# Load times in a planner's model, the place of an operand split, and when weights are decoded

## The chip, the cores and the metric

The kernel runs on one core of a Trainium2 chip. The metric is device time in microseconds (us), less is better. TensorE (PE) multiplies and transposes through PSUM, VectorE (DVE), ScalarE (ACT) and GpSimd (POOL) do elementwise work, SyncE (SP) issues DMAs. Each engine takes its instructions in the order in which the program lists them, and each instruction waits for the semaphores of what it needs.

## What is computed

A recurrence over 768 steps for 4 x 8 heads with a 40x40 state, then two feed-forward layers on its 3072 x 320 output:

```python
for t in range(S):
    y[:, :, t] = np.einsum('bhd,bhde->bhe', rt, state)
    Sa = np.einsum('bhde,bhe->bhd', state, at)
    state = state * wt[:, :, None, :] - np.einsum('bhd,bhe->bhde', Sa, bt) + np.einsum('bhd,bhe->bhde', vt, kt)
# first layer: h = x @ w_in (320 x 1024); softmax times h; layer norm; @ w_out (1024 x 320)
# second layer: h = x @ w_in (320 x 2048); g = max(h, 0) + alpha * min(h, 0); g @ w_out (2048 x 320)
```

The weights of both layers come as 64-bit floats.

## The kernel before

**Two parts.** The recurrence runs in 24 slots `g`, each a chunk of 32 steps of all heads; two chunks make one of 12 windows `w`. Slot g does `stage_x`, `stage_u`, `stage_st`, `stage_s` for its chunk and `stage_uf`, `stage_g2`, `stage_y` for the one before. For every four slots a triangular inverse is prepared: `gen1` (matmuls `pg`, masks into `XS`), 28 small dependent VectorE steps between transposes (`inverse`), then two groups of small matmuls (`pv`, `pn`). `slot_tasks` puts the last of it into the slot with c4 = g % 4 = 3. The first layer follows three and four slots behind the recurrence, from a queue of small pieces: `mm1` (16 pieces of `h`), `tr1`, `mm2` (8 pieces of `po`), `tr2`. After slot 23 comes a tail, ordered by the string TAIL, which finishes the first layer while the second layer runs for window 0 (`s` is a step of it, `w` loads weights, `n t u a b o` are pieces of the first layer). The last part runs the second layer for windows 1 to 11 in six groups of two windows (the last has one): per pair of steps `mm3` (`ph`), VectorE `gt`, ScalarE `gh`, POOL `gll`, and `mm4` (`acc`) two steps later.

**The order is written by a planner.** While the program is built, a model keeps a time `now[0]` for TensorE and one for each of ScalarE, VectorE and POOL (`free`). `note` advances TensorE's time by a booked price. `until` waits in the model for a key: meanwhile it pops pieces of the first layer from the queue, or filler matmuls (`zero`, in the early slots `busy`), whose product nobody reads. `pace` adds such work where the matmul columns of the last stretch are few. `fill` gives VectorE work from five lists when it is free in the model. Loads are booked as landed `DMA` = 3.5 us after they are asked for. The resulting order is kept on PE, ACT, DVE and POOL in the slots; SP's order is not written by the planner.

**Decoding of weights.** `w1_tasks` (11 pieces) and `w2_tasks` (28) load a piece of 64-bit words into a tile `raw` of a pool of two buffers (line 912). `decode_steps` turns it into fp32: VectorE masks (lines 877, 878), ScalarE conversions (881, 882), VectorE sign and low word (885, 889), then a product on VectorE or POOL (898), and for the second layer a store to `wd` or `od` in DRAM (947), from which `load_w` reads later. `pump` keeps at most two loads ahead and starts a piece when `lane["due"]` allows it: 11 at the start, then per slot NC[g % 4], NL[g % 4] in the last four slots.

**Moves.** `x_move` stores the recurrence's output `Y` to `xd` (line 751) and loads it again as `xt` in the layout of the first layer (752, 753). `tr2` transposes the first layer's output into PSUM, ScalarE rounds it to fp32r (high part), VectorE subtracts (low part, 856 and 857), and the five slices go to `x2_d` with one store (865). The last part loads them straight into its operand tile (1268).

Of the kernel before, what the change touches and what calls it, by code (L numbers as in the profile page):

```python
# [25 lines left out]
NC, NL = (1, 2, 2, 2), (2, 2, 2, 0)  # L26
# [6 lines left out]
TAIL = "s2 n0 w2 t0 s1 u0 a0 w3 b0 s1 n1 w4 o0 s1 t1 s1 u1 a1 w5 s1 b1 s1 n2 o1 s1 w6 t2 s1 u2 a2 x w7 s1 b2 s1 n3 o2 s1 t3 s1 u3 b3 s2 o3"  # L33
PLAIN_WT = {'gen00': 0.44, 'gen20': 1.8, 'tr1': 0.19}
LAT, PL, DMA = 0.1, 0.25, 3.5
# [10 lines left out]
def tile_kernel(ctx: ExitStack, tc: tile.TileContext, w_fm, a0_fm, a_fm, kb_fm, r_fm, v_fm, v_tm,  # L46
# [26 lines left out]
    x2_d = [dr.tile([128, 5, 256], F32R, name=f"x2d{w}") for w in range(NW)]  # L73
# [86 lines left out]
    st = {}  # L160
# [79 lines left out]
    def note(dt, n, r=0):  # L240
        page[0] += r
        if page[0] >= PAGE and not plain():
            page[0] -= PAGE
            t, page[1] = page[1] + FETCH, max(now[0], page[1] + FETCH)
            while now[0] < t:
                note(min(0.1, t - now[0]), 0)
        now[0] += dt
# [117 lines left out]
    def load_a(g):  # L365
# [8 lines left out]
        put(("a_in", g))(max(now[0], free["P"]) + DMA)  # L374
# [369 lines left out]
    def x_move(w):  # L744
# [7 lines left out]
        nc.sync.dma_start(out=f32(xt[:, 0:4]), in_=xd[w][0:n4].rearrange("(k p) t -> p k t", p=128))  # L752
        nc.sync.dma_start(out=f32(xt[:, 4]), in_=xd[w][n4:])


# [89 lines left out]
    def tr2(t):  # L845
# [6 lines left out]
        x2 = m1.tile([128, 5, 128], F32R, name="x2")  # L852
        hi = x2[:, 0:4, :].rearrange("p (a b) t -> p a b t", b=2)

        def low():
            nc.vector.tensor_tensor(out=hi[:, :, 1], in0=pt[:, 0:2], in1=f32(hi[:, :, 0]), op=ALU.subtract)
            nc.vector.tensor_tensor(out=x2[64:128, 4], in0=pt[0:64, 2], in1=f32(x2[0:64, 4]), op=ALU.subtract)

        def high():
            nc.scalar.copy(out=hi[:, :, 0], in_=pt[:, 0:2])  # L860
            nc.scalar.copy(out=x2[0:64, 4], in_=pt[0:64, 2])

        def end(u):
            wring[bk] = u
            nc.sync.dma_start(out=f32(x2_d[w][:, :, i * 128:i * 128 + 128]), in_=f32(x2[:]))
        chain(now[0] + PL, [("A", 0.64, high), ("V", 0.74, low)], end)


# [39 lines left out]
    def piece(src, dst=None, scales=(), eng="V", end=lambda o: []):  # L908

        n = src.shape[1] * src.shape[2]  # L910
        raw = rawp.tile([128, 1024], U32, name="raw")[:, 0:2 * n]
# [52 lines left out]
    def pump():  # L964

        while lane["tasks"] and lane["taken"] < over() + 2:
            lane["next"].append((lane["tasks"].pop(0)(), now[0] + DMA))
# [266 lines left out]
    def early_w():  # L1234
# [8 lines left out]
        for t, a, z in zip(st["x20"], (0, 4), (4, 5)):  # L1243
            nc.sync.dma_start(out=f32(t), in_=f32(x2_d[0][:, a:z] if z > a + 1 else x2_d[0][:, a]))

    def phase2(p2):
# [18 lines left out]
        def load_x(ws, t):  # L1265
# [378 lines left out]
```

## Time and profile before

| | us |
|---|---|
| median of 3 runs | 1111.93 |
| lowest and highest | 1100.17, 1115.77 |
| profiled execution, device time | 1114.18 |
| its span, first to last instruction | 1112.4 |

| engine | busy us | share of the span |
|---|---|---|
| PE | 1010.7 | 91% |
| PEld (weight loads) | 790.0 | 71% |
| DVE | 653.8 | 59% |
| ACT | 526.5 | 47% |
| POOL | 298.7 | 27% |

A matmul's end is modelled in the profile, so a busy PE is not a PE at its peak. The granted clock is that of TensorE as a share of full speed. An "idle before" names the engine's idle time just ahead of an instruction and what ended it.

### The profile page before, as it was taken

The page shows a single profiled execution, that of the slowest core. Times are in us where ns is not written, and L with a number is a line of the kernel's source. Part 1 is how long each engine was busy: PE and PEld are TensorE (multiplying, and loading weights), DVE is VectorE, ACT ScalarE, POOL GpSimd, SP SyncE. Part 2 cuts the span into 40 slices and gives each one's busy share as a digit, 9 for nine tenths or more (in the row PEclk, how much of TensorE's full clock was granted, in tenths as well). Part 3 has the DMA queues.
Part 4 walks back from the last instruction along what each step waited for, and adds up shares of the span by engine and source line. Part 5 has one row for each costly group of instructions (what it writes and reads, how often), then busy time and mean ns, then how long its engine had stood idle before and what let it go on. Part 6 is the DMA issues. An engine that isn't in the chain of part 4 may idle for free.

```text
span 1112.4 us, 36263 instructions
## 1 busy us (share of the span) xinstructions
PE 1010.7 (91%) x15862; PEld 790.0 (71%) x15862; DVE 653.8 (59%) x1242; ACT 526.5 (47%) x1177; POOL 298.7 (27%) x352
## 2 busy tenths in 40 slices
PE   6589979699879799799999899999999999999997
PEld 3346647476657557666777577688899988999997
DVE  8837977587668677576868353554434443334443
ACT  1226727367567537475667477658412121212121
POOL 6400131012212221122202113143333333333332
PEclk9668979699998899798899899999999999999999
DMA  7504343534453523462453433356202020201010
GB/s 175 161 28 113 81 113 96 132 103 113 147 150 102 151 69 100 116 156 84 112 151 100 142 97 84 94 190 199 59 1 71 1 71 1 72 1 48 1 25 15
DMA packets 103145, 103.55 MB, mean 93 GB/s; under 512 B 37828, under 2 KB 80580, under 8 KB 102980
## 3 DMA queue, kind: packets, MB, share of 16 engines
q1 hardware_dynamic: 102980, 101.16, 33.1%
q8 instruction: 126, 2.06, 0.8%
q14 instruction: 39, 0.32, 0.1%
HBM read 75.71 MB, written 25.43 MB: 91 GB/s over the span
## 4 chain that ended last, share of the span: by engine, by line
PE 68%; DMA 9%; DVE 9%; ACT 6%; issue 5%; POOL 2%; SPq 1%; DVEq 0%; POOLq 0%; ACTq 0%
PE ph L1279 15%; PE po L837 8%; PE h L767 6%; PE acc L1299 5%; PE acc L1297 5%; PE acc L1298 5%; DMA raw<-in_w_out_dram 3%; PE busy L339 3%; PE py L724 3%; PE zero L297 2%; PE pst L665 2%; PE pf L652 2%; PE pg L701 2%; PE pss L685 2%; DMA kbf<-in_kb_fm_dram 2%
## 5 line engine op out<-in xcount | busy, mean ns | idle before, releaser
L802 DVE TENSOR_SCALAR gt<-ph,al 128x512 f32<-128x512 f32 (+1 forms) x112 | 75.3, 674 | 194.3 <-PE ph L1279 194.2
L1286 POOL TENSOR_TENSOR gll<-gt,gh 128x512 fp32r<-128x512 f32 (+1 forms) x112 | 128.2, 1146 | 226.9 <-ACT gh L1285 225.0
L1285 ACT CAST gh<-gt 128x512 fp32r<-128x512 f32 (+1 forms) x112 | 62.4, 558 | 251.3 <-DVE gt L803 215.3
L837 PE MATMUL po<-wo,ln 128*128 128x320 f32 x384 | 131.6, 477 | 0.9 <-ACT ln L829 0.8
L767 PE MATMUL h<-w1h,xt 128*128 128x512 f32 x240 | 94.9, 452 | 0.0
L837 PEld LDWEIGHTS po<-wo,ln 128*128 128x128 f32 x384 | 71.7, 201 | 26.4 <-issue 4.5
L1297 PE MATMUL acc<-w2h,gh 128*128 128x320 f32 x288 | 88.8, 308 | 0.0
L1298 PE MATMUL acc<-w2l,gh 128*128 128x320 f32 x288 | 88.8, 308 | 0.0
L1299 PE MATMUL acc<-w2h,gll 128*128 128x320 f32 x288 | 88.7, 308 | 0.0
L898 POOL TENSOR_TENSOR raw<-em 128x512 f32<-128x512 f32 (+1 forms) x28 | 38.0, 1364 | 128.8 <-issue 64.2
L339 PE MATMUL busy<-busy 128*128 128x512 bf16 x212 | 65.3, 462 | 6.7 <-issue 3.5
L803 DVE SCALAR_TENSOR_TENSOR gt<-ph,gt 128x512 f32<-128x512 f32 (+1 forms) x112 | 68.7, 615 | 3.7
L767 PE MATMUL h<-w1l,xt 128*128 128x512 f32 x144 | 65.2, 453 | 0.0
L578 ACT COPY KBS<-pt 64x160 f32<-64x160 f32 x192 | 55.1, 287 | 17.4 <-PE pt L574 15.1
L1279 PE MATMUL ph<-w1h,w2h 128*128 128x512 f32 x180 | 59.3, 394 | 0.0
L372 POOL MEMSET XS<- 32x512 f32 (+1 forms) x36 | 18.7, 520 | 150.8 <-PE px L614 149.8
L687 ACT COPY KBS<-pss 40x320 f32<-40x320 f32 x92 | 38.4, 417 | 37.3 <-PE pss L685 35.5
L490 ACT ACTIVATE GR<-pg 32x256 f32<-32x256 f32 x96 | 36.1, 376 | 41.0 <-PE pg L479 39.8
L1298 PEld LDWEIGHTS acc<-w2l,gh 128*128 128x128 f32 x288 | 54.1, 188 | 1.4
L1297 PEld LDWEIGHTS acc<-w2h,gh 128*128 128x128 f32 x288 | 54.1, 188 | 1.3
L709 DVE TENSOR_TENSOR YS<-pg,mask 64x256 f32<-64x256 f32 x96 | 40.4, 421 | 24.5 <-PE pg L701 22.6
L877 DVE TENSOR_SCALAR em<-raw 128x512 int32<-128x512 int32 (+1 forms) x39 | 16.3, 419 | 65.2 <-DMA raw<-in_w_out_dram 50.5
(183 smaller groups left out, 2340.1 us busy)
## 6 DMA issues: line engine op xcount, KB each, us to landing
kbf<-in_kb_fm_dram SPq DMA_DIRECT2D x24, 416.0 KB
x2d<-x SPq DMA_DIRECT2D x24, 320.0 KB
raw<-in_w_in_dram SPq DMA_DIRECT2D x14, 512.0 KB
raw<-in_w_out_dram SPq DMA_DIRECT2D x13, 512.0 KB
xd<-Y SPq DMA_DIRECT2D x24, 256.0 KB
xt<-xd SPq DMA_DIRECT2D x12, 512.0 KB
wt<-in_w_fm_dram SPq DMA_DIRECT2D x24, 211.7 KB
VUS<-in_v_tm_dram SPq DMA_DIRECT2D x48, 80.0 KB
```

What stands on the lines that cost most here:

```text
L339: nc.tensor.matmul(st["busy"], lhsT=busy[:, 0:128], rhs=busy, start=True, stop=True)
L578: t = run("A", 0.29, lambda k=k, c=c, r=r, o=o: nc.scalar.copy(out=k[r:r + 64, 1 - r // 64, q * 4:q * 4 + 4, :], in_=pt[64 * c:64 * c + 64 ...
L767: nc.tensor.matmul(st["h"][:, ns], lhsT=l, rhs=r, start=j == 0, stop=j == len(ops) - 1)
L802: nc.vector.tensor_scalar(out=tmp, in0=h, scalar1=0.0, scalar2=al, op0=ALU.min, op1=ALU.mult)
L803: nc.vector.scalar_tensor_tensor(out=o, in0=h, scalar=0.0, in1=tmp, op0=ALU.max, op1=ALU.add)
L837: nc.tensor.matmul(po, lhsT=st["ln", t][:, piece], rhs=wo1[:, piece], start=piece == 0, stop=piece == K1 - 1)
L1279: nc.tensor.matmul(p, lhsT=l, rhs=r, start=j == 0, stop=j == len(ops) - 1)
L1285: nc.scalar.copy(out=gh, in_=t)
L1286: nc.gpsimd.tensor_tensor(out=gll, in0=t, in1=f32(gh), op=ALU.subtract)
L1297: nc.tensor.matmul(acc, lhsT=gh[:, cs], rhs=oh, start=f == 0, stop=False)
L1298: nc.tensor.matmul(acc, lhsT=gh[:, cs], rhs=ol, start=False, stop=False)
L1299: nc.tensor.matmul(acc, lhsT=gll[:, cs], rhs=oh, start=False, stop=f == K2 - 1)
```

## The change

- RAWD = 9.0 is booked instead of DMA = 3.5 for loads of `raw` and for `load_a`; SLOW = 1.1 multiplies the price of every matmul in `note`.
- NC and NL: one decoded piece instead of two in slots with g % 4 = 1 or 3, two in each of the last four slots.
- `pump` keeps four loads ahead for the first ten pieces; of the first eight, the third, fourth, seventh and eighth use the tiles `P` and `ln` of the first layer.
- `x_move` asks for the `xt` loads 3.5 us of the model after the stores. (In the tail, where the model does not run, at once.)
- `x2_d` holds fp32, three slices instead of five. `tr2` only copies (ScalarE) and stores with two DMAs. `parts_in` loads a group into a staging tile, `parts_split` makes the five slices with three ScalarE copies and three VectorE subtractions: for window 0 by a planned event in slot 22, for the first group at the new `y` in TAIL, for later groups after step 6 of the group before.

```diff
-NC, NL = (1, 2, 2, 2), (2, 2, 2, 0)
+NC, NL = (1, 1, 2, 1), (2, 2, 2, 2)
-TAIL = "... w7 s1 b2 s1 n3 o2 s1 t3 s1 u3 b3 s2 o3"
+TAIL = "... w7 s1 b2 s1 n3 o2 s1 t3 s1 y u3 b3 s2 o3"
-LAT, PL, DMA = 0.1, 0.25, 3.5
+LAT, PL, DMA, RAWD, SLOW = 0.1, 0.25, 3.5, 9.0, 1.1
-    x2_d = [dr.tile([128, 5, 256], F32R, name=f"x2d{w}") for w in range(NW)]
+    x2_d = [dr.tile([128, 3, 256], F32, name=f"x2d{w}") for w in range(NW)]
...
+        dt *= SLOW if n else 1.0
         now[0] += dt
...
-        put(("a_in", g))(max(now[0], free["P"]) + DMA)
+        put(("a_in", g))(max(now[0], free["P"]) + RAWD)
...
-        nc.sync.dma_start(out=f32(xt[:, 0:4]), in_=xd[w][0:n4].rearrange("(k p) t -> p k t", p=128))
-        nc.sync.dma_start(out=f32(xt[:, 4]), in_=xd[w][n4:])
+        def load():
+            nc.sync.dma_start(out=f32(xt[:, 0:4]), in_=xd[w][0:n4].rearrange("(k p) t -> p k t", p=128))
+            nc.sync.dma_start(out=f32(xt[:, 4]), in_=xd[w][n4:])
+        later(now[0] + DMA, load)
...
-        x2 = m1.tile([128, 5, 128], F32R, name="x2")
...
-        chain(now[0] + PL, [("A", 0.64, high), ("V", 0.74, low)], end)
+        x2 = m1.tile([128, 3, 128], F32, name="x2")
+        def copy():
+            nc.scalar.copy(out=x2[:, 0:2], in_=pt[:, 0:2])
+            nc.scalar.copy(out=x2[0:64, 2], in_=pt[0:64, 2])
+        def end(u):
+            wring[bk] = u
+            ts = slice(i * 128, i * 128 + 128)
+            nc.sync.dma_start(out=x2_d[w][:, 0:2, ts], in_=x2[:, 0:2])
+            nc.sync.dma_start(out=x2_d[w][0:64, 2, ts], in_=x2[0:64, 2])
+        chain(now[0] + PL, [("A", 0.64, copy)], end)
+    def parts_in(ws, s):
+        for i, w in enumerate(ws):
+            c = slice(i * 256, i * 256 + 256)
+            nc.sync.dma_start(out=s[:, 0:2, c], in_=x2_d[w][:, 0:2])
+            nc.sync.dma_start(out=s[0:64, 2, c], in_=x2_d[w][0:64, 2])
+    def parts_split(x, s):
+        n = x[0].shape[-1]
+        for k in range(2):
+            nc.scalar.copy(out=x[2 * k], in_=s[:, k, 0:n])
+            nc.vector.tensor_tensor(out=x[2 * k + 1], in0=s[:, k, 0:n], in1=f32(x[2 * k]), op=ALU.subtract)
+        nc.scalar.copy(out=x[4][0:64], in_=s[0:64, 2, 0:n])
+        nc.vector.tensor_tensor(out=x[4][64:128], in0=s[0:64, 2, 0:n], in1=f32(x[4][0:64]), op=ALU.subtract)
...
-        raw = rawp.tile([128, 1024], U32, name="raw")[:, 0:2 * n]
+        i = st["piece"] = st.get("piece", -1) + 1
+        raw = (m1.tile([128, 1024], U32, name="raw", tag=("P", "ln")[i % 2]) if i < 8 and i % 4 > 1 else
+               rawp.tile([128, 1024], U32, name="raw"))[:, 0:2 * n]
...
-        while lane["tasks"] and lane["taken"] < over() + 2:
-            lane["next"].append((lane["tasks"].pop(0)(), now[0] + DMA))
+        while lane["tasks"] and lane["taken"] < over() + (4 if lane["taken"] < 10 else 2):
+            lane["next"].append((lane["tasks"].pop(0)(), now[0] + RAWD))
...
-        for t, a, z in zip(st["x20"], (0, 4), (4, 5)):
-            nc.sync.dma_start(out=f32(t), in_=f32(x2_d[0][:, a:z] if z > a + 1 else x2_d[0][:, a]))
+        s = XS[1].rearrange("p a b s t -> p (a b s t)")[:, 0:768].rearrange("p (k n) -> p k n", k=3)
+        parts_in([0], s)
+        a, b = st["x20"]
+        later(now[0] + 2 * DMA, lambda: (run("A", 1.2, lambda: parts_split([a[:, 0], a[:, 1], a[:, 2], a[:, 3], b], s), now[0]),
+                                         run("V", 1.2, lambda: None, now[0])))
...
+            elif x == "y":
+                parts_split(nxt["x"], nxt["s"])
             elif x == "x":
-                nxt = load_x(groups[0], x_tile(0))
+                nxt = load_x(groups[0], x_tile(0), cm.tile([128, 3, 512], F32, name="w1l"))
...
-                nxt = load_x(groups[i + 1], x_tile(i + 1))
+                nxt = load_x(groups[i + 1], x_tile(i + 1), cm.tile([128, 3, 512], F32, name="wo1"))
...
                 step(G, [f, f + 1], d4, LAG)
+                if f == 6 and nxt is not G:
+                    parts_split(nxt["x"], nxt["s"])
```

## Rows read from the trace of the kernel before

**Rows 1.** The page: busy time of engines, and TensorE's granted clock in 40 slices.
```profile
PE 1010.7 (91%) x15862; PEld 790.0 (71%) x15862; DVE 653.8 (59%) x1242; ACT 526.5 (47%) x1177; POOL 298.7 (27%) x352
PEclk9668979699998899798899899999999999999999
```

**Rows 2.** Busy time by stretch: stretch, length, engines (instructions), clock, DMA share, GB/s.
```profile
core 0: us, PE busy (x) PEld busy (x) DVE busy (x) ACT busy (x) POOL busy (x), PEclk, DMA share, GB/s
200.00:225.00 25.00, 15.29 (x186) 9.91 (x186) 15.71 (x29) 7.42 (x16) 2.74 (x4) 0.66 0.40 106
325.00:350.00 25.00, 18.34 (x375) 14.49 (x371) 15.12 (x30) 12.83 (x26) 4.36 (x6) 0.80 0.42 117
350.00:375.00 25.00, 18.92 (x314) 14.47 (x313) 16.45 (x32) 17.31 (x44) 4.34 (x7) 0.87 0.58 165
```

**Rows 3.** TensorE's timeline in slot 11: start, length, line, tiles, count.
```profile
364.61 0.80 PE L614 MATMUL px<-VUS,XS 104*32 104x40 f32 x64
...
396.39 2.54 PE L297 MATMUL zero<-D 104*128 104x512 bf16 x11
...
415.93 0.80 PE L614 MATMUL px<-VUS,XS 104*32 104x40 f32 x64
```

**Rows 4.** Busy time by stretch: slot 21.
```profile
654.30:673.20 18.90, 18.90 (x399) 13.70 (x398) 6.89 (x14) 14.39 (x35) 1.78 (x4) 1.00 0.43 110
```

**Rows 5.** The chain of waits in order of time: start, length, what.
```profile
132.09 3.35 DMA xd<-Y
...
172.56 4.71 DMA raw<-in_w_out_dram
...
196.23 9.90 DMA raw<-in_w_out_dram
...
358.49 4.98 DMA xd<-Y
...
538.45 3.84 DMA raw<-in_w_in_dram
...
728.70 4.31 PE po L837 x16
```

**Rows 6.** Groups by line: count, busy us, mean ns, idle before and what ended it.
```profile
L877 DVE TENSOR_SCALAR em<-raw 128x512 int32<-128x512 int32 (+1 forms) x39 | 16.3, 419 | 65.2 <-DMA raw<-in_w_out_dram 50.5 <-DMA raw<-in_w_in_dram 14.5
```

**Rows 7.** SP's timeline in slot 11.
```profile
363.48 0.38 SPq L752 DMA_DIRECT2D xt<-xd  x1
363.99 0.43 SPq L912 DMA_DIRECT2D raw<-in_w_out_dram  x1
```

**Rows 8.** VectorE's timeline in slot 11, with the idle time before.
```profile
369.08 0.43 DVE L877 TENSOR_SCALAR em<-raw 128x512 int32<-128x512 int32 x1 [7.70 <-DMA raw<-in_w_out_dram]
```

**Rows 9.** TensorE's waits: who waited for whom, us in total, times, longest.
```profile
PE pst L665 <- ACT VUS L634: 9.4, 3, 8.7
...
PE pss L685 <- DVE VUS L670: 6.2, 1, 6.2
...
PE pf L652 <- ACT XP L617: 5.6, 1, 5.6
```

**Rows 10.** The chain of waits in slot 15: a store ahead of a load.
```profile
519.65 4.10 DMA od<-raw
```

**Rows 11.** Busy time on tile `em` over the span: DVE, ACT, POOL.
```profile
0.00:1112.00 1112.00, 82.40 (x174) 42.77 (x78) 38.04 (x28) 0.93 0.34 93
```

**Rows 12.** Busy time on tile `x`, which `tr2` writes: DVE, ACT.
```profile
0.00:1112.00 1112.00, 16.84 (x48) 12.71 (x48) 0.93 0.34 93
```

**Rows 13.** Waits of SP's queue: who waited for whom, total, times, longest.
```profile
SPq L865 <- DVE x L857: 78.9, 19, 13.2
```

**Rows 14.** Groups by line: a VectorE subtraction of 128x512.
```profile
L928 DVE TENSOR_TENSOR w1l<-raw,w1h 128x512 fp32r<-128x512 f32 x6 | 4.1, 688 | 4.4 <-ACT w1h L934 4.4
```

**Rows 15.** Busy time by stretch: the last part.
```profile
800.00:825.00 25.00, 25.00 (x144) 22.87 (x144) 10.10 (x14) 4.79 (x8) 9.95 (x8) 1.00 0.00 1
```

**Rows 16.** TensorE's timeline after its longest idle time.
```profile
218.00 3.60 PE L297 MATMUL zero<-D 104*128 104x512 bf16 x8
```

More of the change, by code (lines that the diff above doesn't have):

```diff
@@ L32 @@
 DA, KP = (1,), (1,)
-TAIL = "s2 n0 w2 t0 s1 u0 a0 w3 b0 s1 n1 w4 o0 s1 t1 s1 u1 a1 w5 s1 b1 s1 n2 o1 s1 w6 t2 s1 u2 a2 x w7 s1 b2 s1 n3 o2 s1 t3 s1 u3 b3 s2 o3"
+TAIL = "s2 n0 w2 t0 s1 u0 a0 w3 b0 s1 n1 w4 o0 s1 t1 s1 u1 a1 w5 s1 b1 s1 n2 o1 s1 w6 t2 s1 u2 a2 x w7 s1 b2 s1 n3 o2 s1 t3 s1 y u3 b3 s2 o3"
 PLAIN_WT = {'gen00': 0.44, 'gen20': 1.8, 'tr1': 0.19}
-LAT, PL, DMA = 0.1, 0.25, 3.5
+LAT, PL, DMA, RAWD, SLOW = 0.1, 0.25, 3.5, 9.0, 1.1
 NCH, CHAT = 8, (4, 10)
@@ L851, in tr2 @@
             nc.tensor.transpose(pt[0:n, q, :], xs[:, q * 128:q * 128 + n], ident)
-        x2 = m1.tile([128, 5, 128], F32R, name="x2")
[L853 to L861, printed above, removed]
+        x2 = m1.tile([128, 3, 128], F32, name="x2")
+        def copy():
+            nc.scalar.copy(out=x2[:, 0:2], in_=pt[:, 0:2])
+            nc.scalar.copy(out=x2[0:64, 2], in_=pt[0:64, 2])
         def end(u):
             wring[bk] = u
-            nc.sync.dma_start(out=f32(x2_d[w][:, :, i * 128:i * 128 + 128]), in_=f32(x2[:]))
-        chain(now[0] + PL, [("A", 0.64, high), ("V", 0.74, low)], end)
+            ts = slice(i * 128, i * 128 + 128)
[14 more added lines that the diff above has]
+        nc.vector.tensor_tensor(out=x[4][64:128], in0=s[0:64, 2, 0:n], in1=f32(x[4][0:64]), op=ALU.subtract)
     def decode_steps(raw, e, m, o, scales=(), eng="P"):
@@ L1263, in parts, with load_x @@
                     for a, b in st["w2", j]]
-        def load_x(ws, t):
-            for i, w in enumerate(ws):
-                c = slice(i * 256, i * 256 + 256)
-                nc.sync.dma_start(out=f32(t[:, 0:5, c]), in_=f32(x2_d[w][:]))
-            return {"x": [t[:, i, 0:256 * len(ws)] for i in range(5)], "n": 256 * len(ws), "ws": ws, "g": {}}
+        def load_x(ws, t, s):
+            parts_in(ws, s)
+            return {"x": [t[:, i, 0:256 * len(ws)] for i in range(5)], "n": 256 * len(ws), "ws": ws, "g": {}, "s": s}
         def mm3(G, fs, sp):
```

## The prediction

> **What bounds the kernel now.** I read the page first: busy shares, then the slices [rows 1]. TensorE is busy 91% of the span, so the tempting answer is "TensorE bound". The row of its granted clock denies half of it: nines in the last third, but sixes to eights among them before. The stretches say the same in numbers [rows 2]: 200 to 225 us has 15.3 us of TensorE work at clock 0.66, 325 to 350 has 18.3 at 0.80, 350 to 375 has 18.9 at 0.87. So what can be won lies in the recurrence slots, before about 635 us. I delimit a slot by its `px` block: slot 11, of the fourth kind (c4 = 3), runs from 364.6 to 415.9 us, 51.3 us [rows 3]; slot 21 takes 18.9 us, with TensorE busy in all of it [rows 4].
>
> Then the chain of waits, in order of time [rows 5]. It is mostly TensorE, but twelve of its pieces are DMAs that belong to the weight decoding or to `x_move`: eight loads of `raw` (4.71, 9.90, 5.91, 4.42, 3.30, 5.00, 3.72, 3.84: 40.8 us; the first two and the last stand in the rows), three `xd` stores (3.35, 5.01, 4.98: 13.3 us; first and last) and one `od` store (4.10 us). Together 58.2 us. The groups by line show where these loads bite: the first decode instruction, VectorE `em<-raw` at L877, has 65.2 us of idle time before it in 39 instructions [rows 6].
>
> One case in full, slot 11. On SP's queue `xt<-xd` starts only at 363.48, when the `xd` store that it reads has landed (358.49 + 4.98 on the chain); right behind it, at 363.99, comes a `raw` load [rows 5, 7]. VectorE has its L877 instruction next and stands 7.70 us before it, until 369.08 [rows 8]. Queued behind it are the `XS` masks and all 28 steps of the inverse, so TensorE first idles (5.6 us before `pf`, [rows 9]) and at the slot's end stretches `pv` and `pn` with `zero` blocks, from 396.39 to 415.93 [rows 3]. The planner had booked 3.5 us from asking for a load to its landing.
>
> **The change, part by part.** The profiled execution took 1114.18 us (span 1112.4), 0.2% above the median of 1111.93; I sum against 1114.2.
>
> *RAWD = 9.0, and `xt` loads asked for 3.5 us after the stores.* Both remove the stall just shown: decoding is ordered on VectorE 9 us after its load was asked for, and `raw` loads no longer stand behind `xt<-xd`. Is 9 enough? Where a buffer is reused the decoded piece must be stored before the next load: 4.10 us for an `od` store [rows 10], then a load of 3.3 to 5.9 us. That is 7.4 to 10, so 9 covers most and 3.5 covered none. What is won: at most the 58.2 us. What TensorE visibly lost to three of the stalls is 8.7 + 6.2 + 5.6 = 20.5 us of idle time [rows 9], and the clock in those same stretches [rows 2] cost (1-0.66) x 15.3 + (1-0.80) x 18.3 + (1-0.87) x 18.9 = 5.2 + 3.7 + 2.5 = 11.4 us. I take 20.5 + 11.4 = 32 us, between the ends; the low end is a third of the 40.8, 14 us, if the next wait stands close behind. Late next is the inverse on VectorE. `load_a` is booked with the same 9 us; its stalls are not counted.
>
> The Trainium skill (DMA: Bandwidth & Descriptors, Anatomy of one DMA) fits a DMA on GpSimd's queue at 2.0 us plus bytes over 436 GB/s: an estimate of 3.2 us for 512 KB. By that 3.5 us was already right, this part wins nothing, and the sum would be 1112 us, the far end of rival A. The loads on the chain disagree: 3.3 to 9.9 us.
>
> *NC and NL.* Before, 11 + 28 pieces are done by slot 19; now 11 + 20 + 8, two in each of slots 20 to 23. A piece is 82.4/39 = 2.1 us of VectorE, 42.8/39 = 1.1 of ScalarE and 38.0/28 = 1.4 of POOL [rows 11]. Slots of the second and fourth kind lose one piece. For four slots of the long fourth kind I count 2.1 us, and 0.7 us of removed split (below): 11 us of VectorE, half of it on the path, as VectorE sets only part of such a slot: 5 won, between 0 and 11. Slots 20 to 23 run on TensorE alone, with VectorE at 6.9 and ScalarE at 14.4 of 18.9 us [rows 4]; each gains 2 x 2.1 - 0.7 = 3.5 us of VectorE and 2.2 of ScalarE. That hides unless an instruction stands in a queue that TensorE waits for: I take 1 us a slot, 4 lost, between 0 and, without the cover, 8 x (2.1 + 1.1) = 26.
>
> *The split of x2 moved to the last layers.* Removed in the slots: two VectorE subtractions per tile, 48 with 16.8 us in all, 0.7 us a slot [rows 12]. The `x2d` store, now two issues, then waits for ScalarE only, where SP stands 78.9 us behind VectorE's `x` [rows 13]. Added: one split for window 0 before the slots end and six in the last part, each three ScalarE copies and three VectorE subtractions of at most 128x512, at no more than the 0.69 us of `w1l<-raw,w1h` [rows 14]: 2.1 us on either engine. In the last part TensorE is busy 25.0 of 25 us and VectorE 10.1 [rows 15]; a group of about 58 us has room for 2.1. Cost 0; not hidden it is 6 x 2.1 = 13 us. The staging tiles take over `w1l`, `wo1` and `XS1` once these are done with, and `y` in TAIL stands ahead of a copy that `b3` needs: taken as 0, at most 2.
>
> *Four raw buffers at first.* Six pieces must be decoded before the first layer's matmuls start in slot 3, and their loads came in pairs. Two more in flight: 3 won, between 0 and the 4.71 us of the earliest `raw` load on the chain.
>
> *SLOW = 1.1.* No work changes, only which matmul stands where in TensorE's order: a wait is filled with a tenth fewer pieces. At full clock the old figures were right: eight `po` pieces (two passes each) take 4.31 us, 0.54 each, booked 0.55 [rows 5]. So 1.1 suits the throttled stretches and is too long elsewhere, where it leaves up to a tenth of a filled wait empty. The 19.5 us of `pv`, `pn` and `zero` in slot 11 show how long such a wait can be [rows 3]: a tenth is 2 us. I take 2 lost in all; the ends are 4 won (fewer `zero` blocks on the path) and 20 lost, were each of slots 1 to 20 to lose 1 us.
>
> Sum: -32 - 5 - 3 + 4 + 2 = -34; 1114.2 - 34 = **1080 us**.
>
> **The rivals.** *A, the wait is handed on.* The chain names only the last releaser; what remains may be nearly as late. Then the low end, 14 us, is won, nothing from NC, and 8 are lost by the late pieces and the new order: 1108 us. For it: the slots of the fourth kind hold 28 dependent inverse steps whatever the loads do. Against it: VectorE stood 7.70 us with that very work behind the load [rows 8].
>
> *B, slower: waits that fillers covered become idle time, and the clock goes.* Place: slots 4 to 19, where most now run at the high level. In the stretch after the 8.7 us of idle time a `zero` matmul takes 3.60/8 = 0.45 us, in slot 11 2.54/11 = 0.23 [rows 3, 16]: 1.2 against 2.4 GHz. If each of the sixteen gets a stretch like 325 to 350, which costs 3.7 us [rows 2], 59 are lost against the 40 won: 1114 + 19 = 1133 us. It decides once eleven slots do so. For it, low clock follows idle time in [rows 2, 9]; against it, no row shows that a tenth fewer is too few.
>
> The Trainium skill (TensorE: Matmul & The Clock Gate, What's actually happening) calls the throttled state the default, which activity releases; that speaks against ordering fewer fillers, and the trace agrees as far as the 0.66 after 8.7 us of idle time goes.
>
> *C, the whole chain share comes back*, because the order at last suits the real loads: 58 + 5 + 3 - 4 = 62 won, 1052 us.
>
> **How the numbers follow.** Forecast 0.57 (1064 to 1098), A 0.20, B 0.10, C 0.13. Two per cent is about what a measurement of this kernel can tell from no change: 22 us, 1090 and 1134. Faster: C, and 0.47 of the forecast: 0.60. Same: the rest of the forecast (0.10), A (0.20), and the part of B below 1134 (0.03): 0.33. Slower: 0.07. The range is 1050 to 1112: it leaves out B and the ends of A and C, under 2 in 10.
>
> **What will show it.** Right: the idle time before L877 falls from 65 us to under 20; no `raw` load over 3 us is left on the chain; in SP's queue no `raw` load stands behind an `xt` load that waits; slots of the fourth kind shrink by some 7 us each; 200 to 225 and 325 to 375 lose their low clock. Slots 20 to 23 may grow by 1 us each, and TensorE stays without gaps in the last part. The forecast is wrong if L877's idle time goes but slots keep their lengths (A), if the clock falls in slots that had 1.00 (B), or if TensorE waits for VectorE's `gt` in the last part.

## The result, and the profile of the changed kernel

The changed kernel takes 1039.78 us (median of four runs, 1035.85 to 1047.79) where the kernel before takes 1106.61 in the same batch: a ratio of 0.940, 95% interval 0.930 to 0.950. That is 67 us won where 34 were forecast, and below the range's low end of 1050. The two profiled executions are further apart, 1114.18 and 1035.85 us, spans 1112.4 and 1034.1: what is read from this pair is 78 us, some 11 more than the medians are apart.

The page first, busy time and the granted clock in 40 slices, as in [rows 1]:

```profile
PE 963.8 (93%) x15773; PEld 765.6 (74%) x15792; DVE 654.7 (63%) x1215; ACT 535.7 (52%) x1198; POOL 305.0 (29%) x352
PEclk8689989998999999999999999999999999999998
```

TensorE does 89 matmuls fewer in 47 us less busy time. All 89 are filler, 63 `zero` and 26 `busy`, and 35 of the 47 us are theirs (lines further down). The rest is the same work in less time, and the clock row says why: where [rows 1] has eleven digits under 9, among them three sixes and two sevens, six are left, with one six and no seven. The stretches of [rows 2] again, then the last slot before the tail (slot 22) and a piece of the last part (columns as in [rows 2]):

```profile
core 0: us, PE busy (x) PEld busy (x) DVE busy (x) ACT busy (x) POOL busy (x), PEclk, DMA share, GB/s
200.00:225.00 25.00, 24.59 (x483) 18.26 (x482) 16.40 (x38) 17.17 (x42) 4.02 (x7) 1.00 0.25 67
325.00:350.00 25.00, 23.83 (x712) 18.16 (x711) 22.77 (x49) 16.46 (x39) 9.71 (x10) 1.00 0.56 152
350.00:375.00 25.00, 24.21 (x649) 18.19 (x649) 16.41 (x31) 16.87 (x38) 6.50 (x10) 1.00 0.37 97
592.00:611.70 19.70, 19.70 (x404) 14.36 (x403) 10.52 (x22) 15.63 (x35) 2.75 (x5) 1.00 0.42 104
850.00:875.00 25.00, 25.00 (x140) 22.47 (x139) 11.12 (x16) 5.06 (x9) 8.37 (x7) 1.00 0.00 1
```

All three stretches stand at 1.00 (0.66, 0.80, 0.87 before). Slot 22 has VectorE at 10.5 us, as the late pieces should make it, and TensorE without a gap. Groups by line, first the filler of the kernel before:

```profile
L297 PE MATMUL zero<-D 104*128 104x512 bf16 x160 | 44.6, 411 | 0.6 <-ACT KBS L578 0.6
L339 PE MATMUL busy<-busy 128*128 128x512 bf16 x212 | 65.3, 462 | 6.7 <-issue 3.5 <-DVE busy L1192 1.8 <-POOL busy L1162 1.3
```

Then the changed kernel, for [rows 6] and for the filler:

```profile
L890 DVE TENSOR_SCALAR em<-raw 128x512 int32<-128x512 int32 (+1 forms) x39 | 15.8, 406 | 5.6 <-DMA raw<-in_w_out_dram 2.9 <-DMA raw<-in_w_in_dram 2.6
L298 PE MATMUL zero<-D 104*128 104x512 bf16 x97 | 24.1, 380 | 0.1
L340 PE MATMUL busy<-busy 128*128 128x512 bf16 x186 | 51.2, 422 | 6.3 <-issue 2.6 <-DVE busy L1207 2.3 <-POOL busy L1177 1.3
```

The first decode instruction waits 5.6 us in all instead of 65.2, and `zero` falls from 160 matmuls with 44.6 us to 97 with 24.1. On the chain of waits (start, length, what), where eight `raw` loads stood, there is one (the 8.30 us of `issue` are time in which the profile shows nothing that POOL waited for):

```profile
604.34 8.30 issue
613.74 3.78 DMA wd<-raw
617.58 4.03 DMA raw<-in_w_out_dram
```

It is a late piece, in slot 23, behind the store of the piece before. The three `xd` stores and the `od` store are gone from the chain, and a `VUF` load of 4.33 us (at 298.36) is new on it. Gone too is an `XS` load of 8.24 us (at 442.84 before) that `load_a` issues and the prediction had left out. In the kernel before VectorE stood behind it:

```profile
451.18 0.69 DVE L462 TENSOR_TENSOR XS<-XS,H 40x512 f32<-40x512 f32 x1 [7.41 <-DMA XS<-in_a_fm_dram]
```

By slots: 0 to 3 took 129.6 us and take 114.7. Slots 4 to 19 by kind: c4 = 0, 93.2 to 81.3; c4 = 1, 117.7 to 94.1; c4 = 2, 90.2 to 94.0; c4 = 3, 166.3 to 132.8. Slots 20 to 22: 55.8 to 56.4. Slot 23 with the tail: 91.1 to 91.9. The last part: 329.7 to 330.5.

**A second ledger: work and clock.** Every run lists its span and its mean granted clock. Span times clock is called "work" below: the time that the same run would have taken at full clock, if all of its time at the low clock had halved. The rest of the span is the loss to the clock. This is an account and not a measurement, for TensorE's idle time and its filler are in both. The four runs of the changed kernel have spans of 1034.1, 1034.8, 1041.2 and 1046.0 us at clocks of 0.971, 0.971, 0.965 and 0.960: work is 1004 to 1005 in each, and only the loss differs, 30 to 42 us. So from run to run of this kernel the loss moves alone. The kernel before has 1112.4 x 0.933 = 1037.9 of work and 74.5 of loss in its profiled execution; over 19 later runs the medians are 1032 and 67. In the profiled pair the 78 us are thus 34 of work and 44 of clock; by the medians it is 28 and 34. What went out of the work is filler (above) and idle time: TensorE's idle time in slots 1 to 22 fell from 62.3 to 30.0 us.

Where the clock went can be read in stretches cut at its changes (columns as above). Between 75 and 800 us the kernel before has thirteen stretches at 0.50 (1.2 GHz), 105.8 us together; seven of them:

```profile
146.50:160.20 13.70, 9.52 (x226) 5.56 (x229) 6.90 (x10) 2.25 (x5) 3.42 (x7) 0.50 0.45 121
204.60:221.70 17.10, 12.40 (x173) 8.16 (x174) 13.67 (x27) 6.93 (x14) 2.74 (x4) 0.50 0.30 76
330.90:341.10 10.20, 8.37 (x49) 6.46 (x50) 7.41 (x16) 5.97 (x11) 1.74 (x1) 0.50 0.48 135
402.50:405.90 3.40, 3.40 (x16) 1.17 (x10) 3.34 (x5) 0.24 (x1) 1.76 (x1) 0.51 0.49 146
450.30:464.00 13.70, 11.07 (x111) 8.55 (x112) 9.54 (x21) 4.27 (x10) 1.04 (x2) 0.50 0.45 119
515.20:518.60 3.40, 3.40 (x8) 2.10 (x7) 3.37 (x7) 1.93 (x5) 2.19 (x2) 0.50 0.09 29
621.00:631.20 10.20, 10.20 (x129) 5.93 (x131) 3.78 (x8) 3.26 (x7) 2.33 (x2) 0.50 0.21 73
```

The changed kernel has these four, 20.5 us:

```profile
134.10:137.50 3.40, 3.40 (x10) 2.72 (x9) 3.34 (x8) 2.68 (x5) 3.21 (x5) 0.50 0.66 114
140.90:147.70 6.80, 5.72 (x46) 3.42 (x47) 1.44 (x2) 1.00 (x2) 0.00 (x0) 0.50 0.01 3
239.90:246.70 6.80, 4.78 (x103) 3.66 (x105) 4.65 (x7) 1.67 (x3) 1.07 (x2) 0.50 0.16 44
396.90:400.30 3.40, 3.40 (x11) 2.52 (x10) 3.25 (x4) 1.51 (x5) 1.60 (x1) 0.50 0.63 177
```

At half the clock half of such a stretch is lost, so this is (105.8 - 20.5) / 2 = 43 us, the 44 of the ledger. (Of the 105.8 us TensorE is busy in 89.1.) Only three of the thirteen (204.6, 330.9 and 368.4, the last not shown: 34.1 us) go with the three stalls of [rows 9]. The other ten follow shorter idle times of TensorE, 0.45 to 5.2 us, or begin in them. The 5.2 us, at the stretch that begins at 450.3, are the wait behind the `XS` load above. Seven of the idle times end in `issue`, six of these in runs of small matmuls, like this one at 621.0, in TensorE's timeline (start, length, line, tiles, count, idle time before):

```profile
620.91 0.37 PE L540 MATMUL pv<-VT,GR 16*32 16x16 f32 x12 [2.94 <-issue]
```

### The profile page after: what moved, and what is told of

It reads as the page before. It is cut to its first block, busy times and chain, and to the rows that moved or that the text cites. A ratio compares the mean times of both kernels' runs of the same rounds, so it can differ in the third digit from the quotient of the medians.

```text
span 1034.1 us, 36144 instructions
## 1 busy us (share of the span) xinstructions
PE 963.8 (93%) x15773; PEld 765.6 (74%) x15792; DVE 654.7 (63%) x1215; ACT 535.7 (52%) x1198; POOL 305.0 (29%) x352
## 3 DMA queue, kind: packets, MB, share of 16 engines
q1 hardware_dynamic: 92276, 93.30, 33.5%
## 4 chain that ended last, share of the span: by engine, by line
PE 71%; ACT 10%; DVE 7%; issue 5%; DMA 4%; POOL 1%; SPq 0%; ACTq 0%; POOLq 0%; DVEq 0%
PE ph L1295 16%; PE po L840 8%; PE h L770 8%; PE acc L1315 5%; PE acc L1313 5%; PE acc L1314 5%; PE pst L666 3%; PE py L725 3%; PE pg L702 2%; ACT GR L491 2%; DMA kbf<-in_kb_fm_dram 2%; PE pv L541 2%; PE pn L541 2%; PE pss L686 2%; PE ptr L828 2%
## 5 line engine op out<-in xcount | busy, mean ns | idle before, releaser
L840 PE MATMUL po<-wo,ln 128*128 128x320 f32 x384 | 124.0, 452 | 2.6 <-DVE wo L908 1.6
L840 PEld LDWEIGHTS po<-wo,ln 128*128 128x128 f32 x384 | 66.6, 189 | 25.0 <-DVE wo L908 2.4
L710 DVE TENSOR_TENSOR YS<-pg,mask 64x256 f32<-64x256 f32 x96 | 40.4, 421 | 33.8 <-PE pg L702 31.9
L671 DVE TENSOR_TENSOR VUS<-pst,VUS 40x320 f32<-40x320 f32 x92 | 44.9, 488 | 21.3 <-PE pst L666 19.5
L340 PE MATMUL busy<-busy 128*128 128x512 bf16 x186 | 51.2, 422 | 6.3 <-issue 2.6
L601 POOL MEMSET YS<- 64x512 f32 x44 | 23.9, 542 | 102.9 <-PE py L725 101.7
L1315 PEld LDWEIGHTS acc<-w2h,gll 128*128 128x128 f32 x288 | 54.1, 188 | 0.2 <-POOL gll L1302 0.2
```

The lines of the kernel that those rows point to most:

```text
L840: nc.tensor.matmul(po, lhsT=st["ln", t][:, piece], rhs=wo1[:, piece], start=piece == 0, stop=piece == K1 - 1)
L1315: nc.tensor.matmul(acc, lhsT=gll[:, cs], rhs=oh, start=False, stop=f == K2 - 1)
```

## The experiments

Each kernel ran beside the kernel before. Ratios are to that kernel in the same batch, with 95% intervals; work and loss are medians of that ledger over all runs of a kernel. Reference points: before, work 1032, loss 67; changed, 1004 and 33.

**One part alone, one part undone.** `b_raw9` books the `raw` loads at 9 us in the kernel before, and does nothing else:

```diff
-LAT, PL, DMA = 0.1, 0.25, 3.5
+LAT, PL, DMA, RAWD = 0.1, 0.25, 3.5, 9.0
-            lane["next"].append((lane["tasks"].pop(0)(), now[0] + DMA))
+            lane["next"].append((lane["tasks"].pop(0)(), now[0] + RAWD))
```

> The kernel before with one part of the change: raw loads booked at 9.0 us instead of 3.5 (RAWD in pump alone). Theory L (late loads hold VectorE, and that is most of the gain): the idle time before the first decode instruction falls from 65 us to under 20, and the time falls by 40 us or more, to 1070 or less. Theory O (the price of TensorE's work in the planner, SLOW, gives most, because it changes the order in every slot): the idle time falls alike, but the time by 20 us or less, since the next wait takes over.

1091.48 us, 0.993 [0.988, 0.998]: 8 us won by the ratio, 10 by the medians, so theory L's 40 is missed. Groups by line of its profiled execution, the shortest of its ten (1079.93 us):

```profile
L297 PE MATMUL zero<-D 104*128 104x512 bf16 x230 | 56.8, 387 | 1.5 <-issue 1.5
L877 DVE TENSOR_SCALAR em<-raw 128x512 int32<-128x512 int32 (+1 forms) x39 | 16.2, 414 | 17.4 <-DMA raw<-in_w_out_dram 15.3 <-DMA raw<-in_w_in_dram 2.0
```

48 us of VectorE's idle time are gone, and 29 us of TensorE's in slots 1 to 22 (62.3 to 33.2); but 70 more `zero` matmuls, 12 us, stand in TensorE's order: part of the wait was handed from an unplanned stall to a planned one. Work is 1037, not lower than before; the gain is in loss, 52. In work this is rival A, for this part by itself.

`b_slow` adds the longer matmul times alone:

```diff
-LAT, PL, DMA = 0.1, 0.25, 3.5
+LAT, PL, DMA, SLOW = 0.1, 0.25, 3.5, 1.1
...
+        dt *= SLOW if n else 1.0
```

> The kernel before with SLOW = 1.1 alone. Theory L: within 10 us of before, the stalls of VectorE before its decode instructions stay at 50 us or more. Theory O: 30 us or more faster, TensorE's filler work (zero, 44.6 us) falls by more than a tenth and its idle time in slots 1 to 22 (62 us) falls too.

1105.07 us, 1.003 [0.999, 1.008]. Nothing in sum, but two large terms in it: work 1016 (16 less) and loss 87 (20 more). The idle time before `em` is still 45.1 us. There are 114 `zero` matmuls instead of 160, and the stretches at 0.50 between 75 and 800 us grow from 105.8 to 150.2 us. Rival B's loss of clock is there, met by an equal gain, but not by its route: TensorE's idle time in slots 1 to 22 fell, from 62.3 to 46.0 us.

`a_slow1` undoes it in the changed kernel:

```diff
-LAT, PL, DMA, RAWD, SLOW = 0.1, 0.25, 3.5, 9.0, 1.1
+LAT, PL, DMA, RAWD, SLOW = 0.1, 0.25, 3.5, 9.0, 1.0
```

> The changed kernel with SLOW = 1.0, all else as changed. Theory L: it stays within 10 us of the changed kernel (1040), the idle time before the first decode instruction stays under 10 us. Theory O: it loses 30 us or more, to 1070 or more, with zero blocks back above 35 us.

1082.04 us, 0.981 [0.972, 0.990]: 42 us slower than the changed kernel, as theory O has it, with the loads on time (8.1 us of idle time before `em`) and TensorE idle no longer in slots 1 to 22 (26.8 us, 30.0 in the changed kernel). Work is 1010, loss 68. The stretch 300 to 500 us, of this kernel and then of the changed one:

```profile
300.00:500.00 200.00, 192.01 (x4140) 138.89 (x4137) 139.52 (x278) 121.85 (x284) 41.43 (x61) 0.85 0.42 111
```

```profile
300.00:500.00 200.00, 188.61 (x4557) 141.86 (x4556) 161.66 (x313) 140.55 (x330) 52.97 (x67) 0.99 0.47 120
```

TensorE is busier without SLOW, at 0.85 against 0.99, and gets 417 matmuls fewer done (of all sizes; the two stretches do not hold quite the same work). A larger busy time is here the sign of the slower kernel.

`a_raw35` books the `raw` loads at 3.5 us again in the changed kernel:

```diff
-            lane["next"].append((lane["tasks"].pop(0)(), now[0] + RAWD))
+            lane["next"].append((lane["tasks"].pop(0)(), now[0] + DMA))
```

> The changed kernel with raw loads booked at 3.5 us again, all else as changed (SLOW, later decoding, four buffers at first, deferred xt loads). Theory L: idle time before the first decode instruction comes back to 40 us or more and the time is 35 us or more longer, 1075 or more. Theory O: 15 us longer at most; the deferred xt loads and the slower model already give the loads time.

1061.63 us, 0.963 [0.955, 0.970]; idle before `em` 25.2 us. Work 1009, loss 50. With 22 us it lies between the two theories.

**Why does SLOW pay, and what are NC and the `xt` load worth?** The function `counted` sums the matmul work that the model has put into the recent past, and a guard adds fillers or queued pieces when that is little. With longer modelled matmuls the same work looks thinner, so the guard acts sooner. `a_guard` keeps SLOW but gives the guard back its old view:

```diff
-        return sum(n * min(1.0, max(0.0, b - t) / max(b - a, 1e-6)) for a, b, n in seen)
+        return 1.1 * sum(n * min(1.0, max(0.0, b - t) / max(b - a, 1e-6)) for a, b, n in seen)
```

> The changed kernel, but the planner's guard on matmul density sees 1.1 times the columns, as many as it saw before SLOW stretched the matmuls; the prices in the waits keep SLOW = 1.1. Theory G (SLOW helps because its stretched matmuls make the guard stricter, so that work is spread before the clock falls): the loss to the clock, span times (1 - clock), goes from 33 us to 55 or more, and the time to 1065 or more. Theory P (SLOW helps because waits in the model match the real ones): within 12 us of 1040, loss under 45.

1074.82 us, 0.969 [0.961, 0.977]. Work 1004, as in the changed kernel; loss 69, as in `a_slow1`; 51 `zero` matmuls instead of 97. SLOW's gain in clock thus needs the guard's stricter view. `a_slow1_g` is the counterpart, SLOW = 1.0 with the stricter guard (the factor 1 / 1.1 in the same line):

> SLOW = 1.0 in the changed kernel, but the guard sees the columns divided by 1.1, as strict as in the changed kernel. Theory G: the loss to the clock falls from the 68 us of SLOW = 1.0 to 45 or less and the time from 1082 to 1055 or less. Theory P: it stays above 1070.

1087.14 us, 0.987 [0.980, 0.993]. Loss 57 instead of 68, but work 1028 instead of 1010, with 147 `zero` matmuls: the guard alone buys clock with filler (42.4 us of it, 30.5 in `a_slow1`), and that costs more than it gives, 1087 us against 1082. Theory G's signs, a loss of 45 or less and 1055 us, are missed: the stricter guard is needed, but it is not enough, and what else SLOW does is not shown.

`a_xnow` asks for the `xt` loads at once, behind the stores:

```diff
-        later(now[0] + DMA, load)
+        load()
```

> The changed kernel with the xt loads asked for right after the xd stores, as before. If they held SP's queue and with it the raw loads (theory L): 10 us or more longer, with raw loads issued right behind xt loads and idle time before the first decode instruction above 15 us. If the 9 us of RAWD cover it: within 8 us of 1040.

1045.49 us, 0.948 [0.941, 0.955]. SP's queue waits for the `xd` stores 35.5 us again, as before the change (35.6; 9.3 in the changed kernel), and it hardly matters: work 1009, loss 34.

`a_nc` puts the old NC and NL back:

```diff
-NC, NL = (1, 1, 2, 1), (2, 2, 2, 2)
+NC, NL = (1, 2, 2, 2), (2, 2, 2, 0)
```

> The changed kernel with the decoding of before (NC, NL): all pieces done by slot 19. Theory L (VectorE's decode work is in the way in the long slots): slots of the fourth kind (132.8 us for four) grow by 5 to 15 us in all, slots 20 to 22 (56.4 us) shrink by 2 to 5; 1045 to 1055. The rival, that the new place of the pieces is a large part of the gain: 1065 or more.

1070.16 us, 0.973 [0.965, 0.981]. Work 1022, loss 48. The slots of the fourth kind take 151.3 us together, 132.8 in the changed kernel. Slot 15, by stretch with the `zero` matmuls alone (busy time of TensorE, clock, DMA share, GB/s), of this kernel and of the changed one:

```profile
434.90:480.40 45.50, 15.19 (x54) 0.92 0.46 129
```

```profile
427.00:458.60 31.60, 0.82 (x3) 1.00 0.50 130
```

The 13.9 us between the two slots are filler (14.4 us more): TensorE's order reaches the end of its pieces there and waits for VectorE, which starts three pieces in that slot instead of two. That the second piece is the cause is not shown: the same block of filler stands in slot 7 of `a_raw35` (14.4 us), which has the new NC. VectorE's waits in `a_nc` (total, times, longest) show the loads late again too:

```profile
DVE em L890 <- DMA raw<-in_w_in_dram: 17.0, 5, 6.9
```

**The split, the load parts together, and two harmless shifts.** `a_split` puts the split back into the slots (the old `x2`, `low`, `high` and `load_x`, without `y` in TAIL):

```diff
...
-        chain(now[0] + PL, [("A", 0.64, copy)], end)
+        chain(now[0] + PL, [("A", 0.64, high), ("V", 0.74, low)], end)
...
```

> The changed kernel with the split of before: two VectorE subtractions per tile in the slots, five slices stored. By the prediction's price (0.7 us of VectorE a slot, part of it on the path): 3 to 10 us longer, 1043 to 1050, and the last part (330 us) unchanged within 1 us. If the store that waits for VectorE holds SP's queue and the raw loads again: idle time before the first decode instruction above 15 us and 1055 or more.

1060.33 us, 0.961 [0.953, 0.968]. Work 1009, loss 50; the last part takes 331.1 us with the split in the slots and 330.5 with it there. With 20 us and an idle time before `em` of 6.1 us neither sign of the expectation is met; the `raw` loads were not held. `b_load_slow` makes both load bookings, the later `xt` load and SLOW together in the kernel before, with its old NC, split and two buffers:

> The kernel before with RAWD = 9 for raw and load_a, the deferred xt loads and SLOW = 1.1, but its own decoding times, split and two buffers. If booking and SLOW together are the gain (each alone gave 10 us and nothing): 1065 or less, work at full clock 1020 or less, loss 45 or less. If decoding's new places are needed too (without them the changed kernel took 1070): 1075 or more.

1085.50 us, 0.984 [0.976, 0.991]. Idle before `em` 18.4 us; work 1029, loss 55; slots of the fourth kind 146.4 us.

`a_raw11` and `a_slow108` move a constant of the changed kernel a little, RAWD = 11.0 and SLOW = 1.08. They ask how much of any difference is the part, and how much is the particular order that the planner happens to write.

> The changed kernel with RAWD = 11 instead of 9. Its loads are already in time (5.6 us of idle time before the first decode instruction), so by the stated causes nothing is left to win: within 8 us of 1040. If the time moves by 15 us or more, the order that the planner happens to write weighs as much as any part of the change, and the single parts' shares are good to no better than that.

> The changed kernel with SLOW = 1.08 instead of 1.1. If the gain grows smoothly with SLOW (1082 us at 1.0, 1040 at 1.1): about 1048, loss to the clock about 40 us. If it depends on the order that happens to come out: anywhere from 1040 to 1085.

1068.55 us, 0.967 [0.959, 0.975] (work 1012, loss 53), and 1060.05 us, 0.960 [0.953, 0.966] (1008, 50). Both are 20 us or more behind the changed kernel without having lost any of its parts.

**The buffers, and more shifts.** `a_two` goes back to two buffers and two loads ahead:

```diff
...
-        while lane["tasks"] and lane["taken"] < over() + (4 if lane["taken"] < 10 else 2):
+        while lane["tasks"] and lane["taken"] < over() + 2:
```

> The changed kernel with two raw buffers and two loads ahead from the start. By the prediction 3 us longer (0 to 5) through slots 0 to 4, slots 0 to 3 growing from 114.7 us by as much; the neighbours' spread on top: 1043 to 1070. If the first weights decoded late hold up the first layer: slots 3 to 5 (87.3 us) grow by 10 or more.

1073.87 us, 0.974 [0.967, 0.981]. Work 1023, loss 50. Slot 0 takes 57.9 us (50.3), with 6.8 us more of `busy` filler; slot 5 takes 40.0 (31.9), with 7.7 us more of `zero`. TensorE's timeline in slot 5:

```profile
200.75 0.81 PE L840 MATMUL po<-wo,ln 128*128 128x320 f32 x2 [0.21 <-DVE wo L908]
201.40 6.21 PE L298 MATMUL zero<-D 104*128 104x512 bf16 x28
208.44 1.34 PE L840 MATMUL po<-wo,ln 128*128 128x320 f32 x4 [0.84 <-DVE wo L908]
209.62 7.29 PE L298 MATMUL zero<-D 104*128 104x512 bf16 x33
216.75 1.24 PE L840 MATMUL po<-wo,ln 128*128 128x320 f32 x4
```

Between `po` pieces TensorE does 28 and 33 `zero` matmuls, until a decoded `wo` piece comes out of VectorE at L908. The early pieces are late, and the layer that needs them waits in slot 5, not at the first load.

The shifts: `a_lat` and `b_lat` set LAT, the model's margin behind a wait, to 0.11 in either kernel; `a_strict` makes the guard 5% stricter (the factor 1 / 1.05 in `counted`).

> The changed kernel with LAT = 0.11 instead of 0.10, a change of the planner's order that no stated cause depends on. If the changed kernel is a typical member of its neighbours: within 8 us of 1040. If it is a lucky order among them (RAWD = 11, SLOW = 1.08 and the old split all gave 1060 to 1069): 1055 to 1070, with a loss to the clock of 45 to 55 us instead of 33.

> The changed kernel with the guard seeing the columns divided by 1.05, stricter than SLOW makes it. If density alone decides the clock: low-clock stretches after 75 us fall below the 20.5 us of the changed kernel, work at full clock grows by less than 10 us from 1004: 1035 to 1045. If the order that comes out decides: 1050 to 1075.

> The kernel before with LAT = 0.11. If before is a typical member of its neighbours: 1090 to 1120. If it was a lucky order too: 1120 or more, and the causes are worth more than the neighbours of the changed kernel alone suggest (some 43 us).

`a_lat`: 1050.41 us, 0.951 [0.942, 0.960] (998, 52). `a_strict`: 1057.03, 0.957 [0.951, 0.964] (1008, 49). `b_lat`: 1095.45, 0.994 [0.991, 0.998] (1029, 65).

**The buffers alone, and with NC.** `b_four` gives the kernel before four buffers and four loads ahead; `b_four_nc` the new NC and NL too.

> The kernel before with four raw buffers at first, alone. If the first layer waits in slots 0 to 5 for its decoded weights (undoing this part in the changed kernel brought slot 0 back to 57.9 us and slot 5 to 40.0, work at full clock 19 us up): slots 0 to 5 (190.6 us in before) shrink by 10 or more, work at full clock falls from 1032 by 8 or more. If the buffers pay only with the loads booked right: no change.

> The kernel before with four buffers at first and the decoding later (NC, NL), without RAWD, SLOW, deferred loads or the split. If these two are where the work went (18 and 19 us each when undone): work at full clock 1017 or less, time 1085 or less, though the stalls before the decode instructions stay at 25 us or more. If the booking is needed for them: 1095 or more.

`b_four`: 1088.68 us, 0.987 [0.981, 0.994] (work 1031, loss 55); slots 0 to 5 take 174.6 us instead of 190.6, about what the whole kernel wins; the fall in work that its expectation wanted is not there. `b_four_nc`: 1104.02 us, 1.006 [1.002, 1.011] (1031, 71). In the one order tried, later decoding takes the buffers' gain away. Its idle time before `em` is 19.5 us, without any new booking and without any time won: that idle time can go and the time stay.

**What the shifts say of all the others.** Five orders hold every part of the change: the changed kernel, `a_raw11`, `a_slow108`, `a_lat`, `a_strict`. Their ratios are 0.940, 0.967, 0.960, 0.951, 0.957: mean 0.955, 50 us won. Work lies at 998 to 1012, mean 1006; loss at 33 to 53, mean 47. So about 50 of the 67 us belong to the change (by the medians 26 of work, 1032 - 1006, and 20 of clock, 67 - 47), and the other 17 to this one order, which of the five loses least to the clock. On the side of the kernel before the spread is known from `b_lat` alone, 6 us. Against this spread the undone parts read so: `a_nc` and `a_two` have work of 1022 and 1023, outside it, 16 to 17 us above the mean; `a_slow1` and `a_guard` have a loss of 68 and 69, outside it, 21 above the mean; `a_slow1_g` lies outside in both; `a_raw35`, `a_split` and `a_xnow` lie inside it in both. Each undone part ran in one order alone, so its share is no surer than this spread. Nothing that ran beat the changed kernel.

## Why the prediction was right and wrong

**Right, by its own signs.** The idle time before the first decode instruction fell below 20 us (5.6). In SP's queue no `raw` load stands behind an `xt` load that waits. The three stretches lost their low clock. Slots of the fourth kind shrank by 33.5 / 4 = 8.4 us each, where 7 was said. Slots 20 to 22 grew by 0.6 us in sum, where 3 was said, since the late pieces stay beneath TensorE's work; slot 23 and the tail grew by 0.8. The split costs nothing in the last part, as the prediction's cover said: 330.5 us with it and 331.1 without. The last part kept its pace. TensorE waits once for `gt` there, a sign that was set against the forecast, but for 1.2 us (0.4 before), and with the split put back for 1.6 (`a_split`). On the chain, as in the kernel before:

```profile
725.31 3.72 PE ph L1295 x16
```

The sum was made against a span in which what could be won lay before 635 us, and all of it came from there.

**Wrong in one sign and two readings.** One `raw` load over 3 us is on the chain, the 4.03 us of a late piece. The `x2d` store was to gain by waiting for ScalarE only; it waits about as long as in [rows 13], for the other engine (SP's waits, total, times, longest):

```profile
SPq L864 <- ACT x L859: 74.9, 17, 11.1
```

And the 5.6 us of TensorE before `pf` in slot 11 did not come by VectorE's masks and inverse. On the chain of the kernel before, behind the `raw` load and VectorE's `em`, stands ScalarE's queue, where `XP` is behind two decode conversions:

```profile
369.54 0.72 ACT em L881
370.26 0.52 ACT em L882
370.78 0.47 ACT ln L829
371.25 0.34 ACT XP L617
371.63 1.04 PE pf L652 x16
```

One late load held the order of two engines.

**The step that failed: the clock term of RAWD, 11.4 us.** It was made from three 25 us stretches around the three longest stalls. The page had the whole of it: mean clock 0.933 over 1112.4 us is a loss of 74.5 us. Ten of the thirteen low stretches, 71.7 us long and thus 36 us of loss, lay elsewhere, behind shorter idle times that [rows 9] leave out. One is `load_a`'s, whose stalls were "not counted": 5.2 us of idle time and 11.1 us of busy time at half the clock, some 11 us by the prediction's own price; no run shows it by itself. The loss fell by 34 by the medians, 44 in the profiled pair, three to four times 11.4. With 34 the sum is -57 and the forecast 1057.6 us; with 44, -67 and 1047.6, against 1039.78. All other terms together, 22.5 us, stand against 28 of work (26 by the mean of the five orders). And some 14 of the 34 us are the luck of this order, which no term could hold: its loss is 33, the mean of the five is 47. The low end of the range had the same fault: rival C, 1052 us, counted the chain's DMAs and left the clock out.

**SLOW, 2 us lost, has the wrong sign.** "No work changes, only which matmul stands where" left out that the guard counts in modelled time. Undone, SLOW costs 42 us, 21 of them in loss beyond the mean of the five orders. Its ends, 4 won to 20 lost, held what it does alone (0.3% slower), but by luck: two large terms cancel. Of rival B the loss of clock exists: alone, SLOW takes 20 us of it. In the changed kernel it gives clock back. Which other part makes the difference is not shown; loads on time are not enough, for `b_load_slow` loses 55 us to the clock and `b_raw9`, without SLOW, 52. The sentence of the Trainium skill (TensorE: Matmul & The Clock Gate, What's actually happening) was weighed against fewer fillers; `a_guard` agrees with it, 51 `zero` matmuls and a loss of 69 against 97 and 33. Their number does not decide alone: `a_slow1_g` has 147 and loses 57. And SLOW itself did not thin the fillers: with it there are 97, without it 103, at losses of 33 and 68, so what it changed is where the work stands.

**RAWD and the `xt` load, 32 us, are not separable as one term.** The stall was real and went, but by itself the booking won 8 to 10 us and no work: part of the wait came back as planned `zero` matmuls, as rival A has it. Undone in the full set it costs 22 us by the medians, within the spread of orders. The later `xt` load freed SP's queue (35.5 us of waits to 9.3) and is worth 6 us, within the spread too. The estimate by the Trainium skill (DMA: Bandwidth & Descriptors, Anatomy of one DMA), by which 3.5 us was right already, is not borne out by the idle times: 65.2 to 17.4 us in `b_raw9` by the booking alone. But the time it gave for this part alone, almost nothing, was nearer than 32.

**The buffers, 3 us, and NC, 5 - 4 = 1 us, were too small.** Undone they cost 34 and 30 us, of which 16 to 17 each are work. The buffers' price was read from the first load on the chain, 4.71 us; what they decide is when the first decoded pieces are there, and that is paid as filler in slots 0 and 5 (7.6 and 8.1 us). NC's price was counted as VectorE's time, half of it on the path; undone, it shows in slot 15 as 14 us, one slot's whole wait in `zero` matmuls. As `a_raw35` has such a block with the new NC, how much of it is NC and how much the order is open. Neither is enough without the rest: with the buffers alone work is 1031, with NC too 1031; and the rest isn't enough without them: bookings and SLOW alone give 1029. The `raw` booking isn't the missing partner, for `a_raw35` has work of 1009. SLOW, alone at 1016, may be; `a_slow1`, at 1010 without it, speaks against that.

**What stays open.** Which of the other parts the buffers and NC need to lower the work isn't told apart. Nor is why this order loses 33 us to the clock and its four neighbours 49 to 53. About half of it lies in one place: in three of the four a low stretch begins in slot 11, in or behind the run of `pv` (`a_raw11` 17.1 us, `a_strict` 20.5, `a_lat` 37.5, thus 9, 10 and 19 us of loss, where they lose 20, 16 and 19 more than the changed kernel). The changed kernel and `a_slow108` have none there. The other low stretches begin at many places, and no single wait explains them. The 17 us are told here as the spread of orders, not as the work of a part.

## What to carry to other kernels

Before stalls are priced one by one, work out the whole loss to the clock, span times one minus the mean granted clock, and split every run into work and loss, knowing that idle time and filler are in both: a change can move both, in opposite ways, and a total of nothing then hides two large terms. Parts of a pipeline (when a load is booked, how many buffers there are, where the pieces are spread) paid here only together, so a part's worth is read by undoing it as well as by adding it. And where a planner writes the order, move a constant that shouldn't matter before a part is credited: here that spread was 29 us, more than three of the six parts cost when undone.

## What the runs showed of the hardware

The work is constant to 1 us over runs of one kernel whose times differ by 12 us (1004 to 1005 us in four runs of the changed kernel): what differs from run to run is how long TensorE's clock is down. In 19 runs of the kernel before it is less sharp, work of 1027 to 1036 and loss of 59 to 81.

The clock also falls where the profile shows TensorE busy throughout (the ends of matmuls are modelled). In `a_split` a stretch of 20.5 us at 0.50 begins at 344.80 (columns as in [rows 2]):

```profile
344.80:365.30 20.50, 20.50 (x345) 11.82 (x335) 10.25 (x14) 4.91 (x9) 3.89 (x2) 0.50 0.26 85
```

TensorE is busy in all of it, and no idle time is listed in the stretch ahead of it; what stands there are runs of 16x16 matmuls between single matmuls of 512 columns:

```profile
342.67 0.31 PE L541 MATMUL pv<-VT,GR 16*32 16x16 f32 x16
342.92 0.50 PE L770 MATMUL h<-w1h,xt 128*128 128x512 f32 x1
343.35 0.25 PE L541 MATMUL pv<-VT,GR 16*32 16x16 f32 x8
343.53 0.50 PE L770 MATMUL h<-w1h,xt 128*128 128x512 f32 x1
...
344.81 0.79 PE L770 MATMUL h<-w1h,xt 128*128 128x512 f32 x1
```

The last line shows the clock down in the work itself: 0.79 us for what took 0.50. That the small matmuls are the cause is an inference from such places (`a_raw11`, `a_strict` and `b_lat` have one each within 30 us of it); no run took the `pv` steps away. It is at least not enough: in the changed kernel the `pv` runs of slots 11 and 15 stand between other matmuls too, and the clock stays up:

```profile
335.90:344.30 8.40, 7.23 (x277) 5.03 (x275) 8.20 (x12) 5.58 (x14) 4.72 (x4) 1.00 0.49 146
433.50:444.60 11.10, 9.66 (x286) 6.06 (x284) 8.17 (x12) 5.50 (x14) 4.48 (x4) 1.00 0.45 127
```

Idle time of TensorE that ends in `issue` has a pattern. The page of the kernel before lists a DMA queue that brings instructions (packets, MB, share):

```profile
q8 instruction: 126, 2.06, 0.8%
```

Its 126 packets of 16 KB stand beside 31991 matmuls and weight loads in the trace, some 254 to a packet. Of the twelve idle times of 0.9 us or more that end in `issue` (23.5 us together), eleven end at the same place when TensorE's instructions are counted by 256s (to within one instruction), and 1.2 to 1.6 us after a packet of that queue ended. In the changed kernel all seven do (to within two instructions). So it is likely that TensorE waited there for its next instructions; no run was made to test it. An order that the planner shifts a little shifts what stands at these places too.
